# Splitting the scores and value products of an attention and MoE kernel from an earlier tile on

## The chip, the cores and the metric

The kernel runs on one core of a Trainium2 chip. The metric is the device time in microseconds of one execution. The engines are named as in the profile: PE is TensorE (PEld its weight loads), DVE is VectorE, ACT is ScalarE, POOL is GpSimd, SP is SyncE, which here issues every DMA.

## The reference

Windowed attention with a few global tokens, for 8 batches and 8 heads, 512 local and 32 global positions, head size 64, followed by a "max of three" feed-forward layer over all 8 x 544 tokens. All in float32:

```python
    s_g = scale * np.matmul(q_g, k_all.transpose(0, 1, 3, 2))
    out_g = np.matmul(sm(s_g), v_all)
    s_ll = scale * np.matmul(q_l, k_l.transpose(0, 1, 3, 2))
    mask = np.abs(pos[:, None] - pos[None, :]) <= window      # window = 32
    s_ll = np.where(mask, s_ll, -1000000000.0)
    s_lg = scale * np.matmul(q_l, k_g.transpose(0, 1, 3, 2))
    a_l = sm(np.concatenate([s_lg, s_ll], axis=-1))
    out_l = np.matmul(a_l, np.concatenate([v_g, v_l], axis=2))
...
    h = np.maximum(np.maximum(x @ w1, x @ w2), x @ w3)        # 4352 tokens, 512 -> 768
    return (h @ w_out).astype(np.float32)
```

Here `sm` is a softmax over the last axis.

## The kernel before

**Tiles.** Heads go in pairs p (0 to 31, four per batch). A tile is 128 local queries of both heads of a pair, so each pair has 4 tiles and the program 128, walked by one loop over `sl`. `ORDER` gives the walk: in the first 16 tiles (batch 0) the first half of the sequence of all four pairs comes ahead of the second half ("by halves"), and from 16 on pair by pair. A tile's keys are a window of 192 or 224 columns (tiles t = 0 and 3 of a pair, or 1 and 2), global keys included.

**Steps of a tile.** `scores` (L347 or L351) makes the score products into the PSUM tile S, DVE scales and masks them with the row minimum (L354), ACT takes the exponential (L356), DVE the sum and its reciprocal (L358, L359), `times` (L116, L118 or L120) multiplies, and from tile 16 on a DMA (L363) moves the result into one of two `prob` tiles. `trans` (L375) transposes these on PE into T, and T is copied to `pt`. `transg` (L393) does the same for the global rows, which `glob` (L290 or L294) scores twice per pair. `pv` (L419 or L426) multiplies by the values into O, and the sum goes to `xr`.

**Two ways of a product.** Unsplit, operands are float32 as they come: L347 for scores, L290 for global scores, L419 for value products. Split, each operand is a high part in float32r and the remainder, also float32r: `split_q`, `split_k` and `split_v` make one cast (`copy`, L105 on DVE or L107 on ACT) and one subtraction (`sub`, L99 on DVE or POOL) for each piece, `qs` and `vs` of 128x256 per tile, `kst` of two pieces of 64x576 and a small `qgz` per pair. Then L351, L294 and L426 do the products with the parts side by side. For a split value product `pt` needs its low part too (L99 from T and from S), and O is taken up in four steps: a copy `lox`, L432, and L434 twice, in place of one copy to `xr`. `NATK` holds the tiles whose scores are unsplit (and the pairs whose global scores are), `NAT` is the first tile with split value products.

**Feed-forward.** `moe_group` yields after each matmul (L465 into pm, six h tiles of three products each, then L484), and `fill(n)` places n of them between a tile's steps: 18 per tile from tile 16 on. Batch 0 is done in two groups of 256 tokens, the first from tile 8 on, the second behind it up to tile 31; later batches have 512 tokens, from tile 32 on. The second group's L465 products stand at tiles 18 to 29, L484 of the first at tiles 16 and 17.

**Weights.** 24 pieces come as float32 and are split on the chip: a load `wraw` (L153, three buffers), L158 on ACT, L161 on POOL, L165 to L167 on DVE in the PSUM tile W, L170 on ACT (high part) and L173 on POOL (low part: wl, and wol for the last six). `WS` gives how many steps of this line follow each tile; the last stand behind tile 17. W and the unsplit value products' O lie in the pool `psE`; the first split value product closes it and opens `psO`, a PSUM tile of two banks.

**What sets the order.** `least` and `settle` keep a ledger of estimated work of ACT, DVE and POOL, and each copy, subtraction and multiplication goes to the engine with the least. The tile framework then schedules the instructions of each engine, so their order differs from the program's, and each engine and SP's queue runs its own order strictly. The buffers that matter: two `prob` tiles, two `kst`, one `kraw` (one key load waits for its split), two `qraw`, one T, one O, two S.

Of the kernel before, what the change touches and what calls it, by code (L numbers as in the profile page):

```python
# [21 lines left out]
NP = H // 2  # L22
# [1 line left out]
KW = 576  # L24
NEG = -8.0e9

NATK = range(0, 28)
NS = 4 * B * NP
ORDER = [4 * p + 2 * h + t for h in range(2) for p in range(4) for t in range(2)] + list(range(16, NS))
HIMAX = float(np.array(0x47EFFFFF, np.int32).view(np.float32))  # L30
# [20 lines left out]
def f32(ap):  # L51
    return ap.bitcast(F32)


def body(ctx, tc, kin, qin, vin, min_, win, out):
# [33 lines left out]
    def settle(ns):  # L89
        top = max(load.values()) - ns  # L90
        for e in load:
            load[e] = max(load[e], top)

    def sub(out, a, b, psum=False):
        n = width(out)
        c = {"d": n * 1.04 + (160 if psum else 110)}
        if not psum:
            c["p"] = n * 2.32 + 130
        (dve if least(c) == "d" else pool).tensor_tensor(out=out, in0=a, in1=b, op=ALU.subtract)  # L99

    def copy(out, a, psum=False):
        n = width(out)
        c = {"d": n * (1.04 if psum else 0.52) + (160 if psum else 150), "a": n * 0.833 + (150 if psum else 190)}
        if least(c) == "d":
            dve.tensor_copy(out=out, in_=a)  # L105
        else:
            act.copy(out=out, in_=a)  # L107
# [88 lines left out]
        weight_load()  # L196


    NAT = 26
    EARLY = 16  # L200
    kraw, kst, qraw, qs, vraw, vs, xr, sc, pg, pts, pgt = [{} for _ in range(11)]
    prob = []
# [18 lines left out]
    def load_k(p):  # L221
        if p < B * NP:
            if 4 * p in NATK:
                kraw[p] = att.tile([128, KW + 2 * SG], F32, name="kn", tag="kst")
            else:
                kraw[p] = att.tile([128, KW + 2 * SG], F32, name="kraw", bufs=1)
            nc.sync.dma_start(out=kraw[p], in_=kin[p])

    def split_k(p):
        if p >= B * NP or 4 * p in NATK:  # L230
            return
        r = kraw.pop(p)
        g = r[:, KW:].rearrange("p (j g) -> p j g", j=2)
        t = qgz
        copy(t[:, :, 0:SG], g)
        sub(t[:, :, 64:64 + SG], g, f32(t)[:, :, 0:SG])
        t = kst[p] = att.tile([128, 2, KW], F32R, name="kst")
        copy(t[0:64, 0], r[0:64, 0:KW])
        copy(t[64:128, 1], r[64:128, 0:KW])
        sub(t[64:128, 0], r[0:64, 0:KW], f32(t)[0:64, 0])  # L240
        sub(t[0:64, 1], r[64:128, 0:KW], f32(t)[64:128, 1])

    def load_q(s):
        if s >= NS:
            return
        if s < EARLY:
# [4 lines left out]
            return  # L251
        if s in NATK:
            qraw[s] = att.tile([128, 256], F32, name="qn", tag="qs", bufs=4)
# [4 lines left out]
    def split_q(s):  # L258
        if s < NS and s not in NATK:
            r = qraw.pop(s)  # L260
            t = qs[s] = att.tile([128, 2, 256], F32R, name="qs", bufs=4)
            copy(t[:, 0], r)
            sub(t[:, 1], r, f32(t)[:, 0])
# [7 lines left out]
    def split_v(s):  # L271
        if NAT <= s < NS:
            v = vraw.pop(s)
            t = vs[s] = att.tile([128, 4, 2, D], F32R, name="vs")
            copy(t[:, :, 0], v)
            sub(t[:, :, 1], v, f32(t)[:, :, 0])

    def glob(p, step):
        if p >= B * NP:
            return  # L280
        if step == 0:
            pg[p] = [att.tile([64, KW], F32, name="sg", bufs=1)[:, 0:NG], small.tile([64, 2], F32, name="nmg"), small.tile([64, 2], F32, name="zg")]
        s, nm, z = pg[p]
        c0, n = SEG[step]
        s0 = 384 * step
        ps = psS.tile([128, 512], F32, name="S")
        if 4 * p in NATK:

            k, g = nat_k(p)
            pe.matmul(ps[0:64, 0:n], lhsT=g, rhs=k[:, c0:c0 + n], start=True, stop=True)  # L290
            in1 = zero[0:64].to_broadcast([64, n])
        else:
            for j in range(2):
                pe.matmul(ps[:, 0:n], lhsT=qgz.rearrange("p j x -> p (j x)")[:, 128 * j:128 * j + 128],  # L294
                          rhs=kst[p][:, j, c0:c0 + n], start=(j == 0), stop=(j == 1))
            in1 = s[:, s0:s0 + n]
            copy(in1, ps[64:128, 0:n], True)
        dve.tensor_tensor_reduce(out=s[:, s0:s0 + n], in0=ps[0:64, 0:n], in1=in1, scale=-0.125, scalar=3.0e38,  # L298
                                 op0=ALU.add, op1=ALU.min, accum_out=nm[:, step:step + 1])
        spend("d", n * 1.04 + 220)  # L300
# [23 lines left out]
    def scores(i):  # L324
# [19 lines left out]
        for j in range(2):  # L344
            if i in NATK:

# [20 lines left out]
    def trans(sl):  # L367
        if sl >= NS:
            return
        s = sc.pop(sl)  # L370
        ps = psT.tile([128, 512], F32, name="T")
        pr, one = (ps, ident) if sl < EARLY else (ps.bitcast(F32R), identr)
        for j in range(2):
            for c in range(2):
                pe.transpose(pr[:, 256 * j + 128 * c:256 * j + 128 * c + 128], s[:, j, 128 * c:128 * c + 128], one)  # L375
        src = ps.rearrange("p (x q) -> p x q", q=128)
        if sl < NAT:
            pt = pts[sl] = att.tile([128, 2, 2, 160], F32, name="pt", tag="pt")
            copy(pt.rearrange("p j c q -> p (j c) q")[:, :, 0:128], src, True)
        else:  # L380
            pt = pts[sl] = att.tile([128, 2, 2, 2, 160], F32R, name="pt", tag="pt")
            v = pt.rearrange("p j c a q -> p (j c) a q")
            copy(v[:, :, 0, 0:128], src, True)
            sub(v[:, :, 1, 0:128], src, f32(v)[:, :, 0, 0:128], True)

    def transg(sl):
# [7 lines left out]
        src = g[:, 64 * h:64 * h + 64 * n].rearrange("p (c j g) -> p c j g", j=2, g=SG)  # L394
        if sl < NAT:
            copy(pt.rearrange("p j c q -> p c j q")[:, 0:n, :, 128:160], src, True)
# [6 lines left out]
    def pv(sl):  # L403
        p, t = divmod(ORDER[sl], 4)
        pt = pts.pop(sl)
        if sl < NAT:
            o = psE.tile([128, 160], F32, name="O")
# [5 lines left out]
        if t == 0:  # L413
            xr[p] = xp.tile([128, 4, 160], F32, name="xr")
        if sl < NAT:

# [78 lines left out]
    def moe_local(b, c0=0, n=SL):  # L495
        def st(t, o):
            r = b * TOK + SG + c0 + t * 128
            nc.sync.dma_start(out=out[r:r + 128], in_=o)
        return moe_group(xs[b], c0, n, st)
# [14 lines left out]
    def fill(n):  # L514
        if mm[0]:
            for _ in range(n):
                next(mm[0], None)
# [3 lines left out]
    def next_scores(last):  # L521
        while ahead[0] <= last:
            scores(ahead[0])
            split_q(ahead[0] + 1)
            load_q(ahead[0] + 4)
            ahead[0] += 1
# [20 lines left out]
    for sl in range(NS):  # L547
        p, t = divmod(ORDER[sl], 4)
        b = p // NP
        settle(4500)  # L550
        if sl == 8:
            mm[0] = moe_local(0, 0, 256)
        elif sl == 16:
            mm[0] = chain(mm[0], moe_local(0, 256, 256))
        elif sl >= 32 and sl % 16 == 0:
            fill(400)
            mm[0] = moe_local(b - 1)
        n = (7, 6, 5, 9) if sl < 16 else (4, 4, 3, 7)
        trans(sl + 1)
        fill(n[0])  # L560
        next_scores(sl + 4 if sl < 12 else max(15, sl + 3))
        if sl >= 16:
            if t == 2:
                split_k(p + 2)
                load_k(p + 3)
        elif sl in (10, 14):
            load_k(sl // 4 + 2)
        elif sl == 15:
            load_k(6)
        fill(n[1])  # L570
        pv(sl)
        if sl < 8:
            if p < 3:
                if t == 0:
                    glob(p + 1, 0)
                    glob(p + 1, 1)
                else:
                    glob_soft(p + 1)
        elif sl < 16:
            if sl in (12, 13):  # L580
                glob(NP, sl - 12)
            elif sl == 14:
                glob_soft(NP)
        elif t <= 1:
            glob(p + 1, t)
        elif t == 2:
            glob_soft(p + 1)
        fill(n[2])
        transg(sl + 1)
        fill(n[3])  # L590
        split_v(sl + 2)
        load_v(sl + 4)
        for _ in range(WS[sl] if sl < len(WS) else 0):
            weight_step()
        if sl < 8:
            if t == 1:
                xs.setdefault(0, []).append(split_x(xr[p][:, 0:2, 0:128]))
        elif sl < 16:
            if t == 3:
                split_x(xr[p][:, 2:4, 0:128], xs[0][p], 256)  # L600
        elif sl % 16 >= 12:
            q = b * NP + sl % 16 - 12
            xs.setdefault(b, []).append(split_x(xr[q][:, :, 0:128]))
# [57 lines left out]
```

## Time and profile before

| what | value |
|---|---|
| median of 3 runs (lowest to highest) | 836.74 us (836.41 to 837.25) |
| the profiled execution: its own time | 835.65 us |
| its span (first to last instruction) | 833.5 us |
| mean granted PE clock | 0.993 |
| instructions | 15973 |
| moved by DMA | 94.56 MB |

Busy times are of one execution and of one engine; a wait is put down to what ended it. Matmuls are pipelined, so a row's duration of one is longer than the time that it takes from the next; the chain of work that ended last gives that time. Matmul records in float32 are two for each instruction of the program, so a tile's four score records of either kind stand for two or for four of the program's products.

### The profile page before, as it was taken

The numbers are of one execution on the slowest core, as the hardware profiler recorded it, in microseconds if no ns is written. First come the engines' busy times: TensorE is split into PE (matmuls) and PEld (weight loads), VectorE is DVE, ScalarE is ACT, GpSimd is POOL, SyncE is SP. The second block draws the span as 40 slices with busy tenths as digits, with TensorE's granted clock in tenths as the row PEclk, the third lists the DMA queues.
The fourth block names the chain that finished last, engine by engine and source line by source line (L and its number), as shares of the span: only waits on it lengthen the run. The fifth ranks groups of instructions, "written<-read, shape, count | busy, mean of one in ns | idle before, by whom it ended". The sixth has DMA issues, their size and how long they took to land.

```text
span 833.5 us, 15973 instructions
## 1 busy us (share of the span) xinstructions
PE 807.3 (97%) x4668; PEld 684.4 (82%) x4668; DVE 522.6 (63%) x1784; ACT 528.3 (63%) x1498; POOL 513.9 (62%) x727
## 2 busy tenths in 40 slices
PE   7789899899999999999999999999999999999997
PEld 5569788878888888888888888888888888888896
DVE  4778735867776767767676776777776776411111
ACT  6688756776776777777776677777677666411210
POOL 4789836886677667867676676866776664311211
PEclk9899999999999999999999999999999999999999
DMA  7567544443334333343335333443335331100001
GB/s 261 175 225 228 183 127 131 137 130 103 105 115 143 114 91 112 105 146 100 103 106 166 107 99 109 120 140 94 95 93 172 109 90 53 59 13 1 26 26 26
DMA packets 93414, 94.56 MB, mean 113 GB/s; under 512 B 18448, under 2 KB 81808, under 8 KB 93328
## 3 DMA queue, kind: packets, MB, share of 16 engines
q1 hardware_dynamic: 93328, 93.56, 36.3%
q8 instruction: 37, 0.61, 0.3%
q14 instruction: 49, 0.40, 0.2%
HBM read 56.85 MB, written 8.91 MB: 79 GB/s over the span
## 4 chain that ended last, share of the span: by engine, by line
PE 83%; DVE 1%; POOL 1%; issue 1%; ACT 1%; DMA 0%; POOLq 0%; DVEq 0%; ACTq 0%
PE pm L465 48%; PE pm L484 16%; PE O L426 6%; PE S L351 5%; PE T L375 4%; PE S L294 2%; PE S L393 1%; PE S L347 1%; PE O L419 1%; DMA prob<-s 0%; ACT s L356 0%; DVE kst L105 0%; POOL s L120 0%; DVE xr L434 0%; DVE sg L298 0%
## 5 line engine op out<-in xcount | busy, mean ns | idle before, releaser
L465 PE MATMUL pm<-xs,wh 128*128 128x512 f32 (+1 forms) x1440 | 422.0, 368 | 5.7 <-ACT xs L107 2.3
L465 PEld LDWEIGHTS pm<-xs,wh 128*128 128x128 f32 x1440 | 253.3, 189 | 36.4 <-ACT xs L107 2.7
L465 PE MATMUL pm<-xs,wl 128*128 128x512 f32 (+1 forms) x720 | 265.1, 368 | 0.2 <-POOL wl L173 0.2
L465 PEld LDWEIGHTS pm<-xs,wl 128*128 128x128 f32 x720 | 136.3, 189 | 20.6 <-issue 1.6
L120 POOL TENSOR_SCALAR s<-s,z 128x224 f32<-128x224 f32 (+1 forms) x246 | 104.9, 438 | 64.8 <-ACT lox L107 40.9
L484 PE MATMUL pm<-woh,h 128*128 128x512 f32 x408 | 133.4, 399 | 0.9 <-POOL h L99 0.9
L99 POOL TENSOR_TENSOR h<-m,h 128x512 fp32r<-128x512 f32 (+1 forms) x60 | 68.6, 1143 | 97.8 <-ACT h L107 97.6
L356 ACT ACTIVATE s<-s,nm 128x224 f32<-128x224 f32 (+1 forms) x256 | 118.1, 462 | 16.5 <-DVE nm L354 12.8
L473 DVE TENSOR_TENSOR m<-pm,m 128x512 f32<-128x512 f32 (+1 forms) x120 | 73.0, 608 | 72.1 <-PE pm L465 71.6
L99 POOL TENSOR_TENSOR qs<-qraw,qs 128x256 fp32r<-128x256 f32 x100 | 73.1, 739 | 62.5 <-ACT qs L107 54.2
L99 DVE TENSOR_TENSOR pt<-T,pt 128x512 fp32r<-128x512 f32 x102 | 70.5, 691 | 62.6 <-ACT pt L107 61.3
L354 DVE CUSTOM_DVE_ANT_0 s<-S,mask 128x224 f32<-128x224 f32 (+1 forms) x240 | 80.7, 371 | 24.5 <-PE S L347 18.0
L484 PEld LDWEIGHTS pm<-woh,h 128*128 128x128 f32 x408 | 74.6, 188 | 13.6 <-POOL h L99 1.5
L484 PE MATMUL pm<-wol,h 128*128 128x512 f32 x204 | 82.1, 403 | 1.2 <-POOL wol L173 1.2
L99 POOL TENSOR_TENSOR kst<-kraw,kst 64x576 fp32r<-64x576 f32 x50 | 71.6, 1432 | 12.9 <-issue 6.2
L99 POOL TENSOR_TENSOR vs<-vraw,vs 128x256 fp32r<-128x256 f32 x102 | 75.4, 740 | 6.3 <-ACT vs L107 3.0
L107 ACT CAST pt<-T 128x512 fp32r<-128x512 f32 x88 | 51.3, 583 | 40.4 <-PE T L375 40.4
L107 ACT CAST qs<-qraw 128x256 fp32r<-128x256 f32 x99 | 40.2, 407 | 53.9 <-PE S L351 50.3
L426 PEld LDWEIGHTS O<-pt,vs 128*128 128x128 f32 x408 | 66.1, 188 | 8.8
L426 PE MATMUL O<-pt,vs 128*128 128x320 f32 (+1 forms) x408 | 72.8, 300 | 0.0
L351 PEld LDWEIGHTS S<-kst,qs 128*128 128x128 f32 x400 | 59.6, 190 | 8.9 <-DVE nmg L298 0.6
L434 DVE TENSOR_TENSOR xr<-O,lox 64x160 f32<-64x160 f32 x204 | 64.3, 315 | 3.4
(97 smaller groups left out, 1222.6 us busy)
## 6 DMA issues: line engine op xcount, KB each, us to landing
vraw<-v_in SPq DMA_DIRECT2D x64, 256.0 KB, 3.1
qraw<-q_in SPq DMA_DIRECT2D x100, 128.0 KB, 2.2
prob<-s SPq DMA_DIRECT2D x56, 224.0 KB, 2.4
wraw<-w_in SPq DMA_DIRECT2D x24, 512.0 KB, 3.6
prob<-s SPq DMA_DIRECT2D x56, 192.0 KB, 2.3
out_dram<-o SPq DMA_DIRECT2D x32, 256.0 KB, 2.5
kraw<-k_in SPq DMA_DIRECT2D x25, 320.0 KB, 3.0
qn<-q_in SPq DMA_DIRECT2D x8, 256.0 KB, 5.6
```

The source lines that it names most:

```text
L99: (dve if least(c) == "d" else pool).tensor_tensor(out=out, in0=a, in1=b, op=ALU.subtract)
L107: act.copy(out=out, in_=a)
L120: pool.tensor_scalar(out=out, in0=a, scalar1=col, scalar2=1.0, op0=ALU.mult, op1=ALU.mult)
L351: pe.matmul(ph[j][:, 0:n], lhsT=qs[i][:, a, 128 * j:128 * j + 128], rhs=kst[p][:, j, c0:c0 + n], start=(a == 0), stop=(a == 1))
L354: dve.tensor_tensor_reduce(out=s[:, j, 0:n], in0=ph[j][:, 0:n], in1=mask[:, (1, 0, 1, 0)[t], 32 * (t == 0):32 * (t == 0) + n], scale=-0.12 ...
L356: act.activation(out=s[:, j, 0:n], in_=s[:, j, 0:n], func=AF.Exp, bias=nm[:, j:j + 1], scale=-1.0, accum_out=ze[:, j, 0:1])
L375: pe.transpose(pr[:, 256 * j + 128 * c:256 * j + 128 * c + 128], s[:, j, 128 * c:128 * c + 128], one)
L426: pe.matmul(o[:, j, 0:320].rearrange("p (a q) -> p a q", a=2)[:, :, 0:n], lhsT=vs[sl][:, 2 * j + c].rearrange("p a d -> p (a d)"), rhs=pt[ ...
L434: dve.tensor_tensor(out=xr[p][64 * j:64 * j + 64, t], in0=o[0:64, j, 0:160], in1=lo[:, j], op=ALU.add)
L465: pe.matmul(ps[:, 0:n], lhsT=w[f][:, i, k], rhs=xs[k][:, a, c0:c0 + n], start=(q == 0), stop=(q == 11))
L473: dve.tensor_tensor(out=m[:, 0:n], in0=ps[:, 0:n], in1=m[:, 0:n], op=ALU.max)
L484: pe.matmul(ps, lhsT=hh[f][:, a, 128 * t:128 * t + 128], rhs=w[:, f], start=(q == 0), stop=(q == 17))
```

## The change

Scores, and global scores, are split from tile 16 (pair 4) on in place of tile 28 (pair 7); value products from tile 18 on in place of 26. Since pairs 4 to 6 now need split keys, the loads and splits of pairs 4 and 5 are placed in the second half of batch 0: pair 4 is loaded at tile 9 and split at 11, pair 5 is loaded at 11 and split at 15, pair 6 loaded at 15.

```diff
-NATK = range(0, 28)
+NATK = range(0, 16)
...
-    NAT = 26
+    NAT = 18
...
             if t == 2:
                 split_k(p + 2)
                 load_k(p + 3)
-        elif sl in (10, 14):
-            load_k(sl // 4 + 2)
-        elif sl == 15:
-            load_k(6)
+        elif sl == 9:
+            load_k(NP)
+        elif sl in (11, 15):
+            split_k(sl // 4 + 2)
+            load_k(sl // 4 + 3)
         fill(n[1])
         pv(sl)
```

`NATK` also tells the host's packing of `q` and of the global queries which layout a tile has.

On PE, around the score of tile 21 and the value product of tile 18 (S and O are the PSUM tiles, pm the feed-forward's):

```order
 L465 MATMUL pm<-xs,wh_98 128x256
-L347 MATMUL S<-kn,qn 128x224 x2
+L351 MATMUL S<-kst,qs 128x224 x4
 L465 MATMUL pm<-xs,wh_98 128x256
 L465 MATMUL pm<-xs,wl_104 128x256
 L465 MATMUL pm<-xs,wh_98 128x256 x2
-L419 MATMUL O<-pt,vraw 64x160 x2
-L419 MATMUL O<-pt,vraw 64x128 x2
+L426 MATMUL O<-pt,vs 128x320
+L426 MATMUL O<-pt,vs 128x2x128
+L426 MATMUL O<-pt,vs 128x320
+L426 MATMUL O<-pt,vs 128x2x128
```

Products are replaced in place, and the feed-forward's stand around them as before.

On POOL, late in the weight conversion, from the zeroing of the first prob tile on; before (L161 and L173 are the conversion's steps):

```order
L338 MEMSET prob 128x512
L173 TENSOR_TENSOR wl_109<-wct,wh_103 128x512
L161 TENSOR_SCALAR wct<-wct 128x512
L173 TENSOR_TENSOR wl_109<-wct,wh_103 128x512
L161 TENSOR_SCALAR wct<-wct 128x512
L99 TENSOR_TENSOR xs<-xr,xs 128x256
L99 TENSOR_TENSOR h_900<-m,h_900 128x256
L173 TENSOR_TENSOR wl_109<-wct,wh_103 128x512
L120 TENSOR_SCALAR s_94<-s_94,z 128x192 x2
L161 TENSOR_SCALAR wct<-wct 128x512
L173 TENSOR_TENSOR wol<-wct,woh 128x512
```

The same place now:

```order
L338 MEMSET prob 128x512
L161 TENSOR_SCALAR wct<-wct 128x512
L99 TENSOR_TENSOR qs<-qraw,qs 128x256 x2
L99 TENSOR_TENSOR kst<-kraw,kst 64x576
L161 TENSOR_SCALAR wct<-wct 128x512
L173 TENSOR_TENSOR wl_109<-wct,wh_103 128x512
L99 TENSOR_TENSOR qs<-qraw,qs 128x256 x2
L173 TENSOR_TENSOR wl_109<-wct,wh_103 128x512
L161 TENSOR_SCALAR wct<-wct 128x512
L99 TENSOR_TENSOR h_900<-m,h_900 128x256
L99 TENSOR_TENSOR xs<-xr,xs 128x256
L173 TENSOR_TENSOR wl_109<-wct,wh_103 128x512
```

Four query subtractions and one key subtraction now stand between the conversion's steps, and the two multiplications of L120 have left for another engine.

On SP, among the last weight loads; before (wraw a weight piece, qn queries of an unsplit tile, prob the softmax; in brackets what the load waits for, DMAHW being earlier DMAs):

```order
L256 DMA qn<-q_in 128x256 [waits PE_49]
L153 DMA wraw<-w_in 128x512 [waits DMAHW5_49,DVE_49,Activation_49]
L268 DMA vraw<-v_in 128x2x256 [waits DMAHW3_49,PE_49]
L153 DMA wraw<-w_in 128x512 [waits DMAHW4_49,DMAHW7_49,DVE_49,Activation_49]
L363 DMA prob<-s_94 128x2x192 [waits Pool_49]
```

The same place now:

```order
L256 DMA qraw<-q_in 128x256 [waits Pool_49]
L256 DMA qraw<-q_in 128x256 [waits DMAHW5_49,Pool_49]
L153 DMA wraw<-w_in 128x512 [waits DMAHW7_49,DVE_49]
L256 DMA qraw<-q_in 128x256 [waits DMAHW4_49,Pool_49]
L256 DMA qraw<-q_in 128x256 [waits DMAHW5_49,DMAHW0_49,Pool_49]
L153 DMA wraw<-w_in 128x512 [waits DMAHW2_49,DMAHW1_49,DVE_49]
L268 DMA vraw<-v_in 128x2x256 [waits PE_49]
L153 DMA wraw<-w_in 128x512 [waits DMAHW3_49,DVE_49]
L363 DMA prob<-s_94 128x2x192 [waits Activation_49]
```

Query loads that waited for PE now wait for POOL, and weight loads stand behind them.

## The prediction

> **What bounds the kernel now.** First the page's line of engine totals, then the windows, since an average over the span hides the stage that the change touches.
>
> ```profile
> PE 807.3 (97%) x4668; PEld 684.4 (82%) x4668; DVE 522.6 (63%) x1784; ACT 528.3 (63%) x1498; POOL 513.9 (62%) x727
> ```
>
> TensorE looks like the bound, the other three like idle hands. By stretches (columns: stretch, length, then busy microseconds of PE, weight loads, DVE, ACT and POOL, granted clock, DMA share):
>
> ```profile
> core 0: us, PE busy (x) PEld busy (x) DVE busy (x) ACT busy (x) POOL busy (x), PEclk, DMA share, GB/s
> 60.00:80.00 20.00, 20.00 (x169) 18.47 (x168) 17.42 (x47) 16.68 (x46) 18.86 (x26) 1.00 0.70 227
> ...
> 67.40:105.00 37.60, 34.52 (x257) 29.52 (x256) 30.15 (x84) 28.66 (x78) 32.30 (x42) 1.00 0.65 204
> ...
> 112.20:138.50 26.30, 26.19 (x215) 23.61 (x214) 12.20 (x62) 14.50 (x48) 13.06 (x21) 1.00 0.45 134
> 138.50:167.00 28.50, 25.56 (x204) 23.72 (x204) 22.49 (x83) 22.66 (x71) 23.45 (x35) 1.00 0.41 125
> 180.00:680.00 500.00, 500.00 (x2771) 424.32 (x2770) 355.59 (x1220) 358.38 (x1016) 349.84 (x486) 1.00 0.38 114
> ```
>
> Add DVE, ACT and POOL and divide by the length. From 180 to 680, with scores and value products split, they work 2.13 busy us per us and PE is never idle. From 112.2 to 138.5, where tiles still go unsplit, it is 1.51 and PE is full. From 138.5 to 167, the first split tiles, it is 2.41 and PE idles 2.94 us; from 67.4 to 105, the end of the weight conversion, it is 2.42 and PE idles 3.08. So PE bounds the kernel except in these two stretches, and the change puts more work for DVE, ACT and POOL into the first of them and into the stage that now has room. One row speaks the other way: 60 to 80 carries 2.65 with PE full.
>
> What PE waits for in the first lossy stretch is the last weight pieces; PE's and POOL's timelines:
>
> ```profile
> 98.97 0.50 PE L484 MATMUL pm<-wol,h 128*128 128x512 f32 x1 [0.68 <-POOL wol L173]
> ...
> 104.55 0.50 PE L484 MATMUL pm<-wol,h 128*128 128x512 f32 x1 [0.48 <-POOL wol L173]
> ```
>
> ```profile
> 103.22 1.28 POOL L173 TENSOR_TENSOR wol<-wct,woh 128x512 fp32r<-128x512 f32 x1 [1.27 <-ACT woh L170]
> ```
>
> The last L173 ends at 104.50, and the product that reads it starts at 104.55. In the second lossy stretch PE's timeline shows transposes waiting for the softmax that returns through a DMA:
>
> ```profile
> 141.75 0.59 PE L351 MATMUL S<-kst,qs 128*128 128x192 f32 x4
> ...
> 145.63 0.51 PE L375 MATMUL T<-identr,prob 128*128 128x128 f32 x4 [0.39 <-DMA prob<-s]
> ...
> 150.20 0.52 PE L375 MATMUL T<-identr,prob 128*128 128x128 f32 x4 [0.78 <-DMA prob<-s]
> ...
> 160.62 0.69 PE L351 MATMUL S<-kst,qs 128*128 128x192 f32 x4 [0.38 <-DVE nmg L298]
> ```
>
> The two score rows are tiles 28 and 32: four tiles in 18.87 us, 4.72 each.
>
> **The change part by part: what PE gains.** The chain that ended last, in order of time, gives what each step takes of PE once the overlap is out. Unsplit, then split:
>
> ```profile
> 111.03 0.76 PE S L347 x4
> ...
> 112.26 0.64 PE O L419 x8
> ...
> 121.27 0.64 PE S L290 x2
> ...
> 126.06 0.27 PE S L290 x2
> ...
> 137.47 0.65 PE S L347 x4
> ```
>
> ```profile
> 180.25 0.35 PE S L294 x2
> ...
> 184.32 0.42 PE S L351 x4
> ...
> 186.27 0.19 PE S L294 x2
> ...
> 190.20 0.44 PE S L351 x4
> ...
> 202.82 0.52 PE O L426 x4
> ```
>
> Twelve tiles' scores (16 to 27) go from 0.76 to 0.44 at width 224 and from 0.65 to 0.42 at 192: 6 x 0.32 + 6 x 0.23 = 3.3 us. The global rows of head pairs 4 to 6 go from 0.64 and 0.27 to 0.35 and 0.19: 3 x 0.37 = 1.1. Eight value products (18 to 25) go from 0.64 to 0.52: 1.0. PE gives back 5.4 us.
>
> **What the other engines pay.** Grouped by form; the last two numbers before the second bar are total us and mean ns:
>
> ```profile
> L99 POOL TENSOR_TENSOR vs<-vraw,vs 128x256 fp32r<-128x256 f32 x102 | 75.4, 740 | 6.3 <-ACT vs L107 3.0 <-DVE vs L105 2.0 <-DVE z L358 1.1
> L99 POOL TENSOR_TENSOR qs<-qraw,qs 128x256 fp32r<-128x256 f32 x100 | 73.1, 739 | 62.5 <-ACT qs L107 54.2 <-DVE nm L354 5.1 <-DVE qs L105 1.2
> L99 POOL TENSOR_TENSOR kst<-kraw,kst 64x576 fp32r<-64x576 f32 x50 | 71.6, 1432 | 12.9 <-issue 6.2 <-ACT kst L107 1.7 <-POOL xs L99 0.9
> L99 DVE TENSOR_TENSOR pt<-T,pt 128x512 fp32r<-128x512 f32 x102 | 70.5, 691 | 62.6 <-ACT pt L107 61.3
> ...
> L434 DVE TENSOR_TENSOR xr<-O,lox 64x160 f32<-64x160 f32 x204 | 64.3, 315 | 3.4
> ...
> L120 POOL TENSOR_SCALAR s<-s,z 128x224 f32<-128x224 f32 x124 | 54.5, 452 | 40.6 <-ACT lox L107 25.8 <-ACT xr L107 6.7 <-ACT pt L107 2.7
> ...
> L432 DVE TENSOR_TENSOR lox<-O,lox 64x320 f32<-64x320 f32 x102 | 49.1, 481 | 17.1 <-ACT lox L107 10.5
> ...
> L107 ACT COPY lox<-O 64x320 f32<-64x320 f32 x100 | 42.3, 423 | 10.3 <-PE O L426 5.1
> ...
> L107 ACT CAST qs<-qraw 128x256 fp32r<-128x256 f32 x99 | 40.2, 407 | 53.9 <-PE S L351 50.3 <-DMA probg<-sg 1.9 <-PE S L347 1.0
> ...
> L107 ACT CAST kst<-kraw 64x576 fp32r<-64x576 f32 x43 | 28.9, 673 | 10.6 <-PE S L351 9.5 <-PE S L347 0.6
> ```
>
> By the counts of the two programs, POOL gets 12 more query subtractions (8.9 us), 4 key ones (5.7) and 8 value ones (5.9), and hands 8 multiplications (3.6) to ACT and DVE: +16.9. ACT gets 13 query casts (5.3), 5 key casts (3.4), 9 copies lox (3.8) and smaller ones. DVE gets 8 subtractions of pt (5.5), 8 of lox (3.8) and 16 of xr (5.0). These rows alone come to 43.7 us for 5.4 of PE. Each is worth nothing where an engine has room; where it stands decides.
>
> *The end of the weight conversion.* Up to the last L173, POOL's order has 7 query subtractions (5.2), 3 key ones (4.3) and 1 value one (0.7) more, and 5 multiplications (2.25) and one 128x256 subtraction (0.7) fewer: +7.2 us ahead of the piece that PE waits for. POOL works 32.30 of the 37.6 us there. With 39.5 to do, the stretch grows by 1.9 if POOL never idles, by 7.2 if all its idle time stays. As full as from 60 to 80 (18.86 of 20) it takes 41.9: **+4.3**, the nearest row. PE's saving here (some 1.4 us) only lengthens its wait.
>
> *Tiles 18 to 25.* Unsplit, tiles 21 to 27 take (137.47 - 111.03) / 6 = 4.41 us each. Split with the same fill of MoE products, 4.72. Eight tiles: +2.5. Tile 20's split score and a global row, where PE is still full, give back 0.3: **+2.2**. Bounds: if PE were the limit, 8 x (0.275 + 0.12 + 0.14) = 4.3 us of saving; if the three engines ran at the 2.65 of the 60 to 80 row in place of 2.41, a tile would take 4.72 x 2.41 / 2.65 = 4.29 and the stage would gain 1.3 in all. I take the measured 4.72, since it comes from the same work per tile with the same fill.
>
> Tiles 26 onward do what they did, at nothing; the stall that now meets the first split tiles moves to tile 16 and is in the 4.3. The earlier key loads cost nothing by themselves: the kraw buffer is free after pair 3's global scores, long before. The PSUM pair of the split products opens at tile 18 and needs the last L167, which stands ahead of the last L173: with that at 109 and tile 18's product some 4 us after its present 112.26, near 116, this too costs nothing; it would if the conversion slipped by 7 us more.
>
> *A rule against it.* One row shows how unlike the same cast can be on DVE (min, median, max ns):
>
> ```profile
> L105 DVE CAST kst<-kraw x7: 457/1344/1640, 120.9 to 618.7; 64x576 fp32r<-64x576 f32 x7
> ```
>
> The Trainium skill, "SBUF — State Buffer", section "Who interferes with whom", says that a VectorE copy in a two-port mode, or a VectorE operation with two SBUF inputs, and a GpSimd operation that reads SBUF shut each other out for the whole instruction; the trace's threefold spread agrees. By that rule alone, as an estimate, the five casts and two key subtractions that DVE gets would each wait for up to one POOL subtraction (0.74 to 1.43 us, say 1.0), 7 us on DVE, or some 2.4 more if shared by the three engines.
>
> **Sum.** 835.65 (the profiled execution; span 833.5 and 2.15 around it) + 4.3 + 2.2 = 842.15. The median of the runs is 836.74, 1.09 above that execution, so 843.2.
>
> **Rivals.** *PE keeps what it gains* (faster): POOL's additions fit into its gaps, the softmax ring keeps pace, and 836.74 - 5.4 = 831.3 comes out. For it: the 60 to 80 row, and 1.51 busy us per us from 112 to 138. Against: that stage would have to carry its own 1.51 x 4.41 = 6.7 us per tile and the split's four to five in 3.9 us, all three engines above 95%. Chance 0.12.
>
> *It evens out*: +1.9 at the weights, -1.3 after: 837.3. Chance 0.12. *Only the weights pay*: +4.3 and -1.3, 839.7. Chance 0.16.
>
> *The load queue turns into the bound* (far slower): SP issues in order, and in its new order four query loads that wait for POOL, and later a key load, stand ahead of weight loads. Such waits exist already further on (total us, times, longest):
>
> ```profile
> SPq L256 <- POOL qs L99: 75.6, 62, 3.3
> ```
>
> If two of the longest reach the weight pieces and through them POOL: 6.6 on top of my sum, 849.8. It decides once POOL starves for pieces, with L158 waiting for wraw. Chance 0.12. That the change doesn't do what it says is no case: the order of PE has 24 native score products fewer.
>
> **How the numbers follow.** My forecast has 0.48. Its bounds are 836.74 + 1.9 + 0.3 at the least and + 7.2 + 2.2 + the 2.4 of the shut-out at the most, 838.9 to 848.5. The range reaches from 836.5, leaving out the PE case and a part of the even one, to 850.0. A measurement can tell about 0.2%, 1.7 us, from no change: faster 0.12, the same 0.12, slower 0.76.
>
> **What would show it.** In the changed profile the last L173 should end near 109 in place of 104.50, with PE's wait for wol above 2 us and POOL over 90% busy from 67 to 109. Tiles 20 to 27 should follow each other at 4.6 to 4.8 us, their transposes waiting for the DMA of prob, with DVE, ACT and POOL near 2.4 together. From tile 32 on all is as before, only later. I am wrong if PE is full between 105 and 165, or if the L173 comes no later than 106.

## The result, and the profile after

The changed kernel takes 846.59 us (median of 4 runs, 845.27 to 847.70), the kernel before 836.93 in the runs beside it (4 runs, 836.41 to 837.25): a ratio of 1.0115, 95% interval 1.0096 to 1.0135, so about 9.7 us slower. The profiled execution of the changed kernel took 847.70 us with a span of 845.9, against 835.65 and 833.5: 12.4 us more of span. That is 2.7 above the difference of the medians: the two profiled executions lie on opposite sides of theirs. The changed kernel's profiled execution is the longest of its four: the two with a mean granted clock of 0.988 took 847.7 and 847.5 us, the two with 0.992 took 845.3 and 845.6.

One correction first: the kernel's description says that the weight pieces come as float32. They come as float64; L158 to L167 make float32 of them, and L170 and L173 then split that. No number of the prediction rests on it.

The changed kernel's page: engine totals, and PE's busy tenths in 40 slices (21 us each).

```profile
PE 807.6 (95%) x4636; PEld 685.7 (81%) x4636; DVE 539.0 (64%) x1824; ACT 546.7 (65%) x1544; POOL 532.2 (63%) x745
...
PE   7788688889999999999999999999999999999997
```

The kernel before, PE's busy tenths:

```profile
PE   7789899899999999999999999999999999999997
```

PE has 32 records fewer than before and yet no less busy time (807.3 then): something ate its saving. Its row is lower than before in slices 4 to 7 and in slice 9, between 63 and 190 us. For the place, I cut at value products that both kernels have: those of tile 11, tile 18 and tile 32. Windows of the changed kernel (length, then busy us of PE, weight loads, DVE, ACT and POOL, granted clock, DMA share):

```profile
core 0: us, PE busy (x) PEld busy (x) DVE busy (x) ACT busy (x) POOL busy (x), PEclk, DMA share, GB/s
60.00:80.00 20.00, 18.10 (x139) 16.54 (x138) 15.12 (x40) 15.91 (x46) 19.23 (x25) 0.91 0.59 196
80.00:100.00 20.00, 14.66 (x110) 13.02 (x108) 13.99 (x38) 13.86 (x39) 16.95 (x22) 0.91 0.62 204
...
68.50:123.30 54.80, 43.15 (x290) 36.44 (x290) 38.95 (x108) 39.47 (x109) 45.25 (x54) 0.91 0.53 171
123.30:192.10 68.80, 61.00 (x449) 55.98 (x448) 53.34 (x201) 54.02 (x163) 52.73 (x77) 1.00 0.44 132
...
192.00:692.00 500.00, 500.00 (x2770) 424.18 (x2769) 354.99 (x1220) 359.71 (x1020) 349.82 (x485) 1.00 0.38 115
```

The kernel before, between the same products:

```profile
68.90:112.20 43.30, 40.22 (x292) 34.05 (x291) 31.44 (x98) 31.67 (x87) 32.43 (x43) 1.00 0.63 196
112.20:179.60 67.40, 63.43 (x480) 56.65 (x480) 43.07 (x173) 44.88 (x140) 46.53 (x68) 1.00 0.44 130
```

Between the value products of tiles 11 and 18 the change costs 54.8 - 43.3 = **11.5 us**; between those of tiles 18 and 32 only 1.4; before and behind nothing (tile 11 comes at 68.5 in place of 68.9, and from 192 PE is full in both). DVE, ACT and POOL together do 123.7 busy us there in place of 95.5, at 2.26 per us in place of 2.21: they were not driven to the 2.65 that 60 to 80 had before. PE's idle time in the stretch is 11.65 us in place of 3.08. And PE is *busy* 2.93 us longer on two records fewer, at a granted clock of 0.91 in place of 1.00. So of the 11.5 us, 8.6 are waiting and 2.9 are longer work of PE.

What PE waited for between the products of tiles 11 and 18 (total us, times, longest), changed kernel:

```profile
PE T L375 <- DMA prob<-s: 3.4, 2, 2.0
...
PE S L351 <- ACT pt L107: 2.9, 1, 2.9
...
PE pm L465 <- ACT m L107: 1.9, 1, 1.9
...
PE O L419 <- ACT pt L107: 1.7, 1, 1.7
...
PE S L393 <- DVE nm L354: 1.0, 1, 1.0
...
PE pm L484 <- POOL wol L173: 0.8, 1, 0.8
```

Their sum is 11.7, all of the idle time. The prediction had put it down to the last of these rows. Six waits that the prediction didn't name stand ahead, on a DMA, ACT and DVE, one or two of each kind. The kernel before, between the same products:

```profile
PE O L419 <- ACT pt L107: 1.2, 1, 1.2
PE pm L484 <- POOL wol L173: 1.2, 2, 0.7
PE T L375 <- ACT xr L107: 0.8, 1, 0.8
```

So the last weight pieces ended only 1.2 of its 3.08 us of waiting. The prediction's reading, that PE waits for them in this stretch, held for that part alone, and their part has become smaller, not larger.

### The profile page after: what moved, and what is told of

It reads as the page before. It is cut to its first block, busy times and chain, and to the rows that moved or that the text cites. A ratio compares the mean times of both kernels' runs of the same rounds, so it can differ in the third digit from the quotient of the medians.

```text
span 845.9 us, 16038 instructions
## 1 busy us (share of the span) xinstructions
PE 807.6 (95%) x4636; PEld 685.7 (81%) x4636; DVE 539.0 (64%) x1824; ACT 546.7 (65%) x1544; POOL 532.2 (63%) x745
## 4 chain that ended last, share of the span: by engine, by line
PE 82%; ACT 5%; DMA 4%; POOL 3%; DVE 3%; issue 2%; SPq 0%; POOLq 0%; ACTq 0%; DVEq 0%
PE pm L465 46%; PE pm L484 16%; PE O L426 7%; PE S L351 5%; PE T L375 4%; DMA wraw<-w_in 2%; DMA prob<-s 2%; PE S L294 2%; ACT s L356 1%; POOL wl L173 1%; PE S L393 1%; DMA qn<-q_in 1%; ACT wct L158 1%; POOL wct L161 1%; ACT pt L107 1%
## 5 line engine op out<-in xcount | busy, mean ns | idle before, releaser
L120 POOL TENSOR_SCALAR s<-s,z 128x192 f32<-128x192 f32 (+1 forms) x238 | 102.5, 443 | 55.4 <-ACT lox L107 45.1
L99 POOL TENSOR_TENSOR h<-m,h 128x512 fp32r<-128x512 f32 (+1 forms) x60 | 68.9, 1148 | 98.2 <-ACT h L107 98.2
L99 POOL TENSOR_TENSOR qs<-qraw,qs 128x256 fp32r<-128x256 f32 x112 | 82.1, 741 | 60.7 <-ACT qs L107 51.6
L99 DVE TENSOR_TENSOR pt<-T,pt 128x512 fp32r<-128x512 f32 x110 | 76.0, 691 | 62.3 <-ACT pt L107 60.8
L99 POOL TENSOR_TENSOR vs<-vraw,vs 128x256 fp32r<-128x256 f32 x110 | 81.8, 744 | 8.2 <-DVE vs L105 3.6
L484 PEld LDWEIGHTS pm<-woh,h 128*128 128x128 f32 x408 | 74.6, 189 | 11.8 <-POOL h L99 0.2
L99 POOL TENSOR_TENSOR kst<-kraw,kst 64x576 fp32r<-64x576 f32 x54 | 77.1, 1427 | 11.2 <-issue 7.2
L107 ACT CAST qs<-qraw 128x256 fp32r<-128x256 f32 x112 | 45.3, 407 | 58.0 <-PE S L351 53.8
L107 ACT CAST pt<-T 128x512 fp32r<-128x512 f32 x96 | 56.1, 584 | 39.1 <-PE T L375 39.1
L426 PE MATMUL O<-pt,vs 128*128 128x320 f32 (+1 forms) x440 | 78.8, 300 | 2.0 <-ACT pt L107 1.2
L351 PEld LDWEIGHTS S<-kst,qs 128*128 128x128 f32 x448 | 66.3, 191 | 13.4 <-ACT pt L107 3.1
L434 DVE TENSOR_TENSOR xr<-O,lox 64x160 f32<-64x160 f32 x220 | 69.4, 315 | 3.6
```

Of the source, the lines that this page charges most:

```text
L120: pool.tensor_scalar(out=out, in0=a, scalar1=col, scalar2=1.0, op0=ALU.mult, op1=ALU.mult)
L351: pe.matmul(ph[j][:, 0:n], lhsT=qs[i][:, a, 128 * j:128 * j + 128], rhs=kst[p][:, j, c0:c0 + n], start=(a == 0), stop=(a == 1))
L426: pe.matmul(o[:, j, 0:320].rearrange("p (a q) -> p a q", a=2)[:, :, 0:n], lhsT=vs[sl][:, 2 * j + c].rearrange("p a d -> p (a d)"), rhs=pt[ ...
L434: dve.tensor_tensor(out=xr[p][64 * j:64 * j + 64, t], in0=o[0:64, j, 0:160], in1=lo[:, j], op=ALU.add)
L484: pe.matmul(ps, lhsT=hh[f][:, a, 128 * t:128 * t + 128], rhs=w[:, f], start=(q == 0), stop=(q == 17))
```

## The experiments

Each run was compared with runs of the kernel before on the same chip. The expectations name theories by letters and state what each gives. "The stretch" is always from tile 11's value product to tile 18's.

**Which edit.** Scores alone, and value products alone (the first as a change to the kernel after, the second to the kernel before):

```diff
-    NAT = 18
+    NAT = 26
```

> Scores split from tile 16 on, value products from tile 26 on as before. Theory A (the loss stands at the end of the weight conversion, from split queries and keys put between its steps on POOL and on the load queue): nearly the whole loss stays, 844 to 846 us, the last L173 near 113 to 115. Theory B (the loss is spread over the split tiles, by the work per tile of scores and value products alike): about half of the loss, 841 to 842 us.

```diff
-    NAT = 26
+    NAT = 18
```

> Value products split from tile 18 on, scores from tile 28 on as before. Theory A: within 1.5 us of the kernel before (836 to 838.5), the last L173 at 104.5 to 106. Theory B: about half of the loss, 841 to 842 us.

The scores alone: 845.53 us, ratio 1.0106 (1.0089 to 1.0124). The value products alone: 837.95, 1.0022 (1.0006 to 1.0038). The stretch of the first, then of the second:

```profile
69.00:123.90 54.90, 42.98 (x292) 36.66 (x291) 39.66 (x109) 38.27 (x105) 43.71 (x53) 0.91 0.54 173
```

```profile
67.70:111.40 43.70, 40.43 (x290) 34.08 (x290) 33.12 (x99) 31.82 (x89) 34.43 (x45) 1.00 0.63 204
```

The whole loss in the conversion stage comes from the scores, with the fallen clock too; eight value products cost 1 us or so.

**Which pairs.** The end of the unsplit scores at tile 20, and at 24; and one step the other way, the kernel before with scores unsplit up to tile 32:

```diff
-NATK = range(0, 16)
+NATK = range(0, 20)
...
-    NAT = 18
+    NAT = 22
```

> Scores split from tile 20 on, value products from 22 on, so that only key pair 5 and no query below 20 is split during the weight conversion. Theory S (the stretch from tile 11's to tile 18's value product goes at about 2.3 busy microseconds of DVE, ACT and POOL per microsecond whichever engine has the work, and its length is the work through that rate): some 12 busy us are added there in place of 28, so 5 us, and 840 to 842 in all. Theory L (what is lost is a fixed upset by early splits, however few): 845 or more.

```diff
-NATK = range(0, 16)
+NATK = range(0, 24)
...
-    NAT = 18
+    NAT = 26
```

> Scores split from tile 24 on, value products from tile 26 on as before: no split stands in the weight conversion. Theory S: the stretch from tile 11 to 18 is as before within 0.7 us, 836 to 838.5 in all. Theory L: as before too, if nothing moves. The rival that split tiles are dear wherever they stand: 839 to 840, a third of the loss.

```diff
-NATK = range(0, 28)
+NATK = range(0, 32)
...
-    NAT = 26
+    NAT = 30
```

> The other way: scores split from tile 32 on and value products from 30 on, in the kernel before. If a split tile with 256-wide feed-forward products around it costs 0.31 us more than an unsplit one, four tiles gain 1.2: 835 to 836.5. If, as tiles 20 to 27 of the changed kernel show (4.54 us against 4.50), it costs nothing net, 836 to 838.

From 20: 841.31, 1.0044 (1.0027 to 1.0060). From 24: 836.78, 0.9998 (0.9987 to 1.0009). From 32: 837.21, 1.0010 (0.9997 to 1.0022). The stretch, from 20 and from 24:

```profile
69.50:116.80 47.30, 41.78 (x290) 35.07 (x289) 36.61 (x106) 34.37 (x94) 40.61 (x51) 0.96 0.54 170
```

```profile
69.40:113.70 44.30, 40.24 (x290) 34.10 (x290) 32.05 (x98) 33.14 (x90) 36.10 (x45) 1.00 0.62 191
```

Split at tile 24 or at 32 the time is that of 28, and from 20 it is the 840 to 842 that theory S gave. Pair 6, whose splits mostly fall behind the conversion, costs nothing in the whole, though the stretch is 1.0 us longer; with pair 5 split the stretch is 4.0 us longer than before, with pair 4 (and value products from 18, which alone cost it 0.4) another 7.5. Where the split stands sets its price.

**Whether the weight loads starve.** In the changed kernel SP's queue waits long between 60 and 130 us, for the query loads' buffers above all, and L158 does wait for wraw between 60 and 122:

```profile
SPq L256 <- POOL qs L99: 17.3, 6, 7.2
...
SPq L256 <- POOL qgz L99: 5.3, 1, 5.3
SPq L227 <- POOL kst L99: 5.1, 1, 5.1
...
ACT wct L158 <- DMA wraw<-w_in: 6.9, 4, 3.4
```

That is what my rival of the load queue had as its sign. Four query buffers in place of two, with the room taken from the output tile:

```diff
-            qraw[s] = att.tile([128, 256], F32, name="qraw")
+            qraw[s] = att.tile([128, 256], F32, name="qraw", bufs=4)
...
-            o = moe.tile([128, 512], F32, name="o", tag="o", bufs=2)
+            o = moe.tile([128, 512], F32, name="o", tag="o", bufs=1)
```

> The changed kernel with four qraw buffers in place of two (and one buffer o in place of two, to make room), so that query loads need not wait for POOL and weight loads behind them on SP are free. Theory Q (the load queue: weight loads stand behind loads that wait for POOL, and ACT waits for the pieces): the waits of L158 for wraw, 6.4 us in the changed kernel, mostly go, the last L173 ends at 111 to 112 in place of 115.2, 842 to 844 us. Theory P (POOL is full, its added 7.2 us are the loss): no change, 845.5 to 847.5 us.

847.59 us, 1.0142 (1.0124 to 1.0161): no gain. The last L173 ends at 112.9 in place of 115.19, but the time that theory Q gave didn't come. L158's wait falls to 0.5; PE's wait for `pt` stays (3.3, in the changed kernel 2.9), and one of 2.7 is new (60 to 122, and the stretch):

```profile
PE S L351 <- ACT pt L107: 3.3, 1, 3.3
...
PE T L375 <- POOL wol L173: 2.7, 1, 2.7
...
ACT wct L158 <- DMA wraw<-w_in: 0.5, 1, 0.5
```

```profile
70.10:121.40 51.30, 42.98 (x291) 36.25 (x291) 39.12 (x107) 38.62 (x108) 42.36 (x52) 0.90 0.57 175
```

The stretch is 3.5 us shorter, but tile 11 comes 1.6 later (70.1 in place of 68.5) and the stage behind, to tile 32 at 190.9, takes 0.7 more. Behind tile 32 it takes 654.7 us, where the changed kernel takes 653.8; one output buffer may be the price there, and no run has that edit alone. The load queue alone falls as the cause.

**Whether POOL is full.** The early query and key subtractions forced onto DVE:

```diff
-    def sub(out, a, b, psum=False):
+    def sub(out, a, b, psum=False, dve_only=False):
...
-        if not psum:
+        if not psum and not dve_only:
...
-        sub(t[:, :, 64:64 + SG], g, f32(t)[:, :, 0:SG])
+        sub(t[:, :, 64:64 + SG], g, f32(t)[:, :, 0:SG], dve_only=p < 6)
...
-        sub(t[64:128, 0], r[0:64, 0:KW], f32(t)[0:64, 0])
+        sub(t[64:128, 0], r[0:64, 0:KW], f32(t)[0:64, 0], dve_only=p < 6)
...
-            sub(t[:, 1], r, f32(t)[:, 0])
+            sub(t[:, 1], r, f32(t)[:, 0], dve_only=s < 23)
```

> The changed kernel with the subtractions of queries 16 to 22 and of key pairs 4 and 5 forced onto DVE, which takes some 10 us of work off POOL up to the last L173. Theory P (POOL is full): the last L173 ends near 106 to 108, 838 to 841 us. Theory Q (the load queue): query loads now wait for DVE, which is behind too; 843 to 846 us.

846.36 us, 1.0124 (1.0109 to 1.0139). The stretch and the stage behind it:

```profile
68.90:119.80 50.90, 42.59 (x291) 36.30 (x290) 41.24 (x108) 36.99 (x102) 40.82 (x50) 0.90 0.52 167
119.80:190.50 70.70, 61.29 (x448) 55.83 (x447) 53.86 (x201) 54.98 (x165) 54.48 (x80) 1.00 0.44 135
```

POOL is 4.4 us lighter and the stretch 3.9 shorter; the stage behind is 1.9 longer, and the total as it was. The last L173 ends at 111.8, not at the 106 to 108 that theory P gave. Two windows show where the relief goes, the changed kernel and then this one:

```profile
70.00:90.00 20.00, 14.78 (x110) 13.12 (x108) 14.86 (x37) 14.20 (x38) 19.30 (x24) 0.91 0.48 160
90.00:110.00 20.00, 14.35 (x93) 12.08 (x94) 15.27 (x40) 15.82 (x43) 14.72 (x19) 0.89 0.64 210
```

```profile
70.00:90.00 20.00, 18.10 (x141) 16.62 (x140) 17.68 (x42) 17.30 (x46) 16.12 (x19) 0.91 0.57 183
90.00:110.00 20.00, 13.59 (x85) 10.94 (x84) 16.91 (x43) 12.48 (x36) 15.81 (x20) 0.88 0.50 161
```

In the changed kernel POOL is full from 70 to 90, 19.30 of 20. With POOL at 16.12, PE's idle time there falls from 5.2 to 1.9 us, so a full POOL may well have had a part in it. From 90 to 110, where POOL was not full, PE idles 6.4 us in place of 5.7. POOL's fullness alone falls as the cause of the whole.

**Both at once.** The two edits together, with the query subtractions on DVE for s < 20 instead of 23:

> Both reliefs at once: the changed kernel with four qraw buffers (one buffer o) and with the subtractions of queries 16 to 19 and of key pairs 4 and 5 on DVE. Each alone shortened the stretch from tile 11's to tile 18's value product by 3.5 to 3.9 of its added 11.5 us. Theory PQ (POOL's fullness and the load queue are two causes, side by side): 47 to 48 us in the stretch in place of 54.8, 839 to 841 in all. Theory C (three engines and the load queue each run a strict order, and relief of one lets the next one hold PE): 50 to 52 in the stretch, and 844 or more in all.

847.77 us, 1.0129 (1.0103 to 1.0155). The total that C expected (844 or more) came; its stretch (50 to 52) not quite:

```profile
71.50:120.70 49.20, 41.00 (x291) 34.16 (x291) 40.42 (x105) 38.25 (x106) 43.01 (x55) 0.97 0.58 181
120.70:191.90 71.20, 62.99 (x447) 57.40 (x447) 52.56 (x197) 51.89 (x159) 53.59 (x79) 0.98 0.43 129
```

The stretch is 5.6 us shorter, but tile 11 comes 3.0 later and tiles 18 to 32 take 2.4 more. The delay has moved to both sides; tile 32 comes at 191.9, after the change it came at 192.1.

**Whether it is the sum of the work.** If the three engines can do some 2.3 busy us per us, a lighter conversion must take the loss away. Four of its steps (L161 and L165 to L167) left out of either kernel, so that the weights are other numbers:

```diff
-        pool.tensor_scalar(out=f32(c), in0=f32(c), scalar1=HIMAX, scalar2=2.0 ** -15, op0=ALU.min, op1=ALU.max)
-        spend("p", 800)
...
-        w = psE.tile([128, 512], I32, name="W")
-        dve.tensor_scalar(out=w, in0=c, scalar1=0x07FFFFFF, scalar2=3, op0=ALU.bitwise_and, op1=ALU.logical_shift_left)
-        dve.scalar_tensor_tensor(out=w, in0=hi, scalar=-0x40000000, in1=w, op0=ALU.bitwise_and, op1=ALU.bitwise_or)
-        dve.scalar_tensor_tensor(out=c, in0=lo, scalar=29, in1=w, op0=ALU.logical_shift_right, op1=ALU.bitwise_or)
-        spend("d", 2000)
```

> The kernel before without four of the seven steps of the weight conversion (L161 on POOL, L165 to L167 on DVE left out, so the weights are other numbers): the ground for the next run. The stretch from tile 11's to tile 18's value product loses some 25 to 30 busy us and becomes bound by PE, near 36 to 38 us in place of 43.3; with the earlier tiles shorter too, 815 to 828 us in all.

> The changed kernel with the same four steps left out. Theory S: the early splits now find room, and the difference from the kernel before with light weights is -2 to +2.5 us in place of +9.7. The rival that early splits cost their time through waits of their own (buffers, load queue, softmax ring), not through the sum of work: +6 us or more remain.

Before, lightened: 825.78 us, 0.9872 (0.9851 to 0.9892). After, lightened: 836.51, 0.9996 (0.9981 to 1.0010). The change costs 10.7 us on top of light conversion too. The stretch of the first, then two windows and the stretch of the second:

```profile
62.30:101.80 39.50, 39.50 (x293) 34.19 (x291) 24.05 (x91) 20.02 (x56) 19.01 (x25) 1.00 0.58 180
```

```profile
60.00:80.00 20.00, 15.63 (x128) 13.94 (x127) 12.36 (x30) 12.59 (x29) 18.29 (x21) 1.00 0.67 223
80.00:100.00 20.00, 15.94 (x112) 14.20 (x113) 15.01 (x56) 10.13 (x32) 10.36 (x13) 0.88 0.37 115
...
63.30:113.00 49.70, 41.27 (x291) 35.03 (x291) 29.64 (x97) 27.59 (x79) 31.77 (x37) 0.93 0.48 153
```

From 80 to 100 PE idles 4 us of 20 while the three engines do only 35.5 of 60, 1.78 per us: nobody is full there, though POOL is from 60 to 80 (18.29 of 20). The sum of work alone falls as the cause. Waits of that kernel between 60 and 122 (its lines behind L161 stand 7 lower: L344 scores, L368 transposes):

```profile
DVE sg L291 <- ACT sg L107: 7.3, 3, 4.8
...
POOL vs L99 <- DVE vs L105: 5.5, 1, 5.5
PE S L344 <- DVE nmg L291: 3.3, 1, 3.3
...
PE T L368 <- DMA prob<-s: 2.9, 2, 1.9
```

Each engine waits for another. One such knot can be read off SP's timeline, where the softmax's way to `prob` stands behind six moves of the global rows:

```profile
88.93 3.71 SPq L315 DMA_DIRECT2D probg<-sg  x6
...
93.39 0.63 SPq L356 DMA_DIRECT2D prob<-s  x1
```

The multiplication whose result this DMA moves (L116 on DVE) had ended at 90.92, and PE's transposes at 95.99 waited 1.88 us for the DMA.

**A longer lead, which told nothing.** Scores a tile earlier, with the key loads a tile earlier too, in the kernel before and after:

```diff
-        next_scores(sl + 4 if sl < 12 else max(15, sl + 3))
+        next_scores(sl + 4)
```

> The kernel before with scores made four tiles ahead of their use from tile 12 on, in place of three (key loads a tile earlier to match). Theory R (the softmax ring: PE waits for transposes because a tile's way from its scores through DVE, ACT, POOL and a DMA takes longer than three tiles give it): PE's idle 6 us from 67 to 167 mostly go, 831 to 834 us. Theory C (the engines' queues are in strict order, and PE waits for whatever stands ahead in them): no gain, 836 to 838.

> The changed kernel with the same lead of four tiles, its key loads and splits a tile earlier. Theory R: the stretch from tile 11's to tile 18's value product falls from 54.8 to 49 us or less, 838 to 842 in all, and the split tiles 20 to 29 run at PE's own 4.2 us. Theory C: 845 to 848, the stretch stays above 53.

1007.65 us (1.2046, 1.2021 to 1.2071) and 1025.92 (1.2273, 1.2226 to 1.2319). The design was bad: with two `prob` tiles, tile sl+4's softmax is written over that of tile sl+2 before it is transposed, so that the output is computed from a successor's softmax, and each transpose waits for a DMA of two tiles later. The kernel before with this lead, waits of its whole span:

```profile
PE T L375 <- DMA prob<-s: 139.5, 94, 3.1
```

94 waits, 139.5 us: in this wrong order the loop hangs on the ring everywhere. What the ring costs in the right order it doesn't show, and between the theories it decides nothing. A lead of four with a third `prob` tile wasn't tried.

## Why the prediction was right, and where it was not

**The sign and the place: right.** The loss stands at the end of the weight conversion, and the split scores of pairs 4 and 5 cause it (scores alone 1.0106, from 24 on 0.9998). The measured 846.6 lies 3.4 above the predicted 843.2. That it lies inside the range is luck in part: the two terms at their upper bounds give 836.74 + 7.2 + 2.2 = 846.1, and the rest is the 2.4 us that the range allowed for the shut-out, which no run measured by itself, and rounding up.

**PE gains 5.4 us: only where PE keeps its clock, and not all of it.** From tile 18 to 32 PE is busy 61.00 in place of 63.43, 2.4 us less, where the prediction's prices give 3.0 (six tiles' scores, one pair's global rows, eight value products). In the stretch ahead of that they give 2.4 (six tiles' scores, two pairs' global rows), and PE is busy 2.9 longer, at the lower clock. PE's timeline of the changed kernel:

```profile
82.25 0.76 PE L419 MATMUL O<-pt,vraw 128*64 128x160 f32 x8
...
90.60 0.70 PE L351 MATMUL S<-kst,qs 128*128 128x224 f32 x4 [2.87 <-ACT pt L107]
...
92.07 1.23 PE L419 MATMUL O<-pt,vraw 128*64 128x160 f32 x8
```

The same eight records take 0.76 us at a granted clock of 1.00 and 1.23 at 0.50. The clock was 0.50 in three spells of the stretch, 10.3 us together; half of that, some 5 us, is an estimate of what they cost, beside the 2.9 + 2.4 = 5.3 by which PE's busy time lies above the prediction's prices. It is a term that I had not reckoned with.

**The conversion's end, +4.3: the step that failed.** It was sized by POOL's fullness: 7.2 us more on POOL ahead of the last L173, as full as 18.86 of 20. The last L173 of the changed kernel, from POOL's timeline, and the product that reads it:

```profile
113.40 1.79 POOL L173 TENSOR_TENSOR wol<-wct,woh 128x512 fp32r<-128x512 f32 x1
```

```profile
115.24 0.50 PE L484 MATMUL pm<-wol,h 128*128 128x512 f32 x1 [0.78 <-POOL wol L173]
```

It ends at 115.19, not near 109; PE's wait for it is 0.78, not above 2; POOL is busy 36.66 of the 42.0 us from 67 to 109, 87%, not above 90. None of the three signs came as named, though the sum has the right sign. +11.5 us stand where the term had +4.3 and its upper bound 7.2 (tile 20's 0.3 apart). The bound itself was wrong. From tile 11's product to the end of the last L173 it takes 46.7 us in place of 35.6, 11.1 more. POOL works 40.07 of them in place of 30.89 and idles 6.6 in place of 4.7: 9.2 us more work, not 7.2, and 1.9 more idle time, where the bound let it stay what it was. Of the extra work 1.9 is one L161 and one L173 more that now stand behind tile 11's product, and 0.5 is the last L173 itself (1.79 us in place of 1.28), which began beside a key subtraction of DVE (112.87 to 114.05).

What the runs put in its place: no one engine's fullness. With POOL lightened, with the loads freed, with both, and with the conversion lightened, the loss stayed at 9.6 to 11.8 us, while the three engines worked at 2.26 per us in the changed kernel, 2.47 with both edits and 1.79 with light conversion. The added instructions stand in strict orders on five queues, and the softmax of each tile goes through all five of them. The time from a tile's first score product to its first transpose, averaged over tiles 12 to 19, was 13.2 us before and 15.8 after (12.5 and 14.6 with light conversion). Relief of one engine moved the wait to the next. This reading agrees with every run, but it is what is left over, not something that a run took away, and POOL's part in it up to 90 us isn't measured by itself.

**The load queue as rival.** Its sign came (L158 waiting for wraw, 6.9 us), its price about as nearly as my own (849.8, 3.2 above the measured), its mechanism didn't hold: without the sign the time is no shorter.

**Tiles 18 to 25, +2.2: too much.** The stage gives +1.4 up to tile 32. First transposes of tiles 20 and 28, changed kernel:

```profile
125.23 0.51 PE L375 MATMUL T<-identr,prob 128*128 128x128 f32 x4
...
161.51 0.46 PE L375 MATMUL T<-identr,prob 128*128 128x128 f32 x4
```

36.28 us for eight tiles, 4.54 each, below the 4.6 to 4.8 that I had named. Before, the first transposes of the same tiles stood at 114.2 and 150.20, 4.50 each: the last two of these already waited for prob, 0.39 and 0.78 us by the rows in the prediction, so that 4.41 held for less than the eight. And 4.72, taken from four tiles only, was too dear for these. The waits named (transposes on the DMA of prob) head PE's list there, but with only 1.6 us from 123.3 to 165. The rate is 2.33 busy us per us, near the 2.4 that I had named.

**No cost from psO, as before from tile 32: held.** Tile 18's value product comes at 123.3, well behind L173; 192 to 692 has PE full.

**Still open:** which shared wait decides, and how much of it is POOL's. Not tried are one output buffer alone, the order of SP with the global rows' moves behind `prob`, a third `prob` tile with a longer lead, and how much of the 2.9 us of PE's slower work comes back once its gaps are closed. None of the kernels that do the whole computation beats the one before: the best, from 24 on, is level with it.

## What to carry to other kernels

Read a stage by all its engines and by what each waits for: if nobody is full and PE still idles, the price of added work is not its duration on one engine, and freeing one engine may only move the wait, as it did here. Find the dose first (here pair 6 cost nothing, pair 5 4 us, pair 4 7.5), since the place of the work told more than four attempts at its cause. An upper bound that keeps idle time as it was, and counts only the instructions added, is no upper bound where strict orders cross.

## What the runs showed of the hardware

*PE's granted clock fell to half for some 3.4 us at a time, behind single waits of 1.9 to 2.9 us.* In the changed kernel's stretch its mean was 0.91 in place of 1.00, from three spells at 0.50: 74.7 to 78.2, 91.8 to 95.2 and 108.8 to 112.2 us. Each began about a microsecond after PE came back from a wait: of 1.90 us (at 73.61), 2.87 (at 90.60) and 1.98 (at 107.78). Waits of 1.42 and 1.65 us in the same stretch (up to 97.55 and 101.78) had no spell behind them. The length of one wait doesn't decide alone: in the changed kernel with light conversion a wait of 3.27 us (up to 76.23) had none behind it, and with one of 1.88 (up to 95.99) the clock fell and stayed at 0.50 to 102. The Trainium skill, "TensorE: Matmul & The Clock Gate", section "What's actually happening", has half rate after an idle window of about 3.4 us. Here the clock fell with waits shorter than that; whether they caused the fall, no run shows.

*A key subtraction on DVE varies twofold.* Changed kernel, then the one with the early subtractions on DVE (min, median, max ns):

```profile
L99 DVE TENSOR_TENSOR kst<-kraw,kst x2: 754/968/1181, 78.3 to 112.9; 64x576 fp32r<-64x576 f32 x2
```

```profile
L99 DVE TENSOR_TENSOR kst<-kraw,kst x4: 942/1248/1582, 72.1 to 103.1; 64x576 fp32r<-64x576 f32 x4
```

The same form takes 0.75 to 1.58 us. That agrees with the shut-out between DVE and POOL that the prediction cites from the Trainium skill, "SBUF — State Buffer", section "Who interferes with whom", though no run here takes POOL's share apart; moving these subtractions off POOL was dearer on DVE than DVE's best row says.
